# A fused retention and max-out kernel on one core: identity products at the start, decay tables loaded later, and another order of the weight conversion

## Chip, cores, metric

The kernel runs on one core of a Trainium2 chip (trn2). The metric is the device time of one execution in microseconds. Most executions of a kernel agree within 0.3%. The granted clock is the share of TensorE's full clock that the profile or the run's record shows; 1.00 is full. Engines are called TensorE (PE in the profile; PEld are its weight loads), VectorE (DVE), ScalarE (ACT), GpSimd (POOL) and SyncE (SP, which issues most DMAs).

## The reference

```python
# q, k, v: (8, 8, 576, 64) float32
scores = 1 / sqrt(64) * q @ k.transpose(0, 1, 3, 2)
gamma  = 1 - 2.0 ** (-5 - arange(8))                  # one decay per head
ret    = scores * where(i >= j, gamma ** (i - j), 0)  # causal, decaying
x      = (ret @ v).transpose(0, 2, 1, 3).reshape(4608, 512)
h      = maximum(maximum(x @ w1, x @ w2), x @ w3)     # w1..w3: (512, 768)
out    = h @ w_out                                    # w_out: (768, 512)
```

The four weight matrices arrive as float64. The kernel loads their bits as integers and assembles float32 from exponent, mantissa and sign.

## The kernel before

It works through 36 chunks of 128 tokens. Each chunk has three steps: `transposes` (k and q), `scores` (q k^T under a mask, and the running state k^T v), and `values`, which ends in `xT`. The program puts TensorE's results into PSUM tiles, and the copy or product by which another engine takes one out is called its eviction; `st` is that of the masked scores, `xT` that of the output products `o`. Four chunks make one token tile of the max-out layer: 18 "up" products with running maxima, then the "down" products with `w_out`. The first tile runs while the weights are still being converted; `convert(n)` records n steps of a generator, and the order of instructions is manual, so the steps stand on each engine exactly where the program has them.

```python
def conversion(piece):                 # 24 pieces of 128 x 512 weights, four steps each
    expo = wtmp.tile(...); mant = wtmp.tile(...)             # two buffers each
    nc.vector.tensor_scalar(out=expo, in0=high, scalar1=0x7FF00000, op0=bitwise_and)   # mask 1
    nc.scalar.activation(mant, low, Identity, bias=one, scale=2.0 ** -52)
    yield
    nc.scalar.activation(expo, expo, Relu, bias=top, scale=-8.0)
    nc.vector.tensor_scalar(out=frac, in0=high, scalar1=0xFFFFF, op0=bitwise_and)      # mask 2
    yield
    nc.scalar.activation(expo, expo, Relu, bias=inf, scale=-1.0)
    nc.vector.scalar_tensor_tensor(out=mant, in0=frac, scalar=2.0 ** -20, in1=mant, ...)   # mantissa
    yield
    nc.vector.scalar_tensor_tensor(out=expo, in0=high, scalar=-2 ** 31, in1=expo, ...)     # sign
    nc.gpsimd.tensor_tensor(w, mant, expo, op=mult)                                        # product
    load_weights(1)
    yield
# ...
def transposes(g):                     # for the first eight chunks
    # ... TensorE transposes k and q into PSUM, then
            if n == "k" and g < CPT:
                nc.vector.tensor_copy(t[:], pt[:])
            else:
                nc.scalar.copy(t[:], pt[:])
# ... order of the program at the start (the decay tables gk, gq, gs were issued first, on ACT):
load(0); load(1); load(2); load_weights(1); load(3); load_weights(2)
decay_values(0); decay_values(1); transposes(0); transposes(1)
decay_values(2); scores(0); transposes(2); values(0)
decay_values(3); scores(1); convert(4); transposes(3); values(1); scores(2)
load(4); values(2); convert(2); scores(3); decay_values(4); convert(2); values(3); convert(4)
# ... then in the first tile, after each of the 18 up products: convert(5 if n < 4 else 4)
```

## Time and profile before

| | before |
|---|---|
| time at first | 861.55 us median of 3 (860.62 to 861.91) |
| span of the profiled run, TensorE busy | 857.7 us, 844.4 us |
| first up product starts | 31.52 us |
| first down product to the second token block's | 108.94 to 121.36 us |

TensorE is full but for two places, the start and the first down products; the prediction shows the views for that. A line of a timeline gives start and length in us, engine, line of the program (line numbers differ between kernels), operation, tiles, shapes and number of instructions, and in brackets the idle time before it and what ended it. A line of waits gives the total in us, the number and the longest. The end of the start in this profile:

```profile
27.51 1.63 PE L208 MATMUL o<-st,vd 128*64 128x128 f32 x16
...
31.52 7.13 PE L370 MATMUL up<-xT,w 128*128 128x512 f32 x16 [0.42 <-DVE xT L215]
```

Also needed are the groups of instructions on VectorE while the first tile is computed (31 to 116 us). Their columns are line, engine, operation, tiles, shapes and count, then busy time and the mean duration in ns, then the idle time before the group and what ended it.

```profile
L269 DVE TENSOR_SCALAR frac<-bits 128x512 int32<-128x512 int32 x22 | 24.8, 1127 | 0.0
L272 DVE SCALAR_TENSOR_TENSOR mant<-frac,mant 128x512 f32<-128x512 int32 x22 | 15.2, 692 | 2.2
L275 DVE SCALAR_TENSOR_TENSOR expo<-bits,expo 128x512 int32<-128x512 int32 x22 | 15.1, 688 | 4.2 <-ACT expo L271 4.2
L264 DVE TENSOR_SCALAR expo<-bits 128x512 int32<-128x512 int32 x22 | 12.5, 567 | 0.0
```

The two mask groups do the same amount of work and should take the same time. The second takes 1127 ns in the mean instead of some 420: most of that is time in which it is started and cannot run.

### The profile page before, as it was taken

What the parts mean: (1) busy time and instruction counts of PE and PEld (TensorE: products, weight loads), DVE (VectorE), ACT (ScalarE), POOL (GpSimd) and SP (SyncE); (2) the same over time, 40 slices, a digit from 0 to 9 for tenths busy, and PEclk for the clock granted to TensorE, in tenths of its full rate; (3) what the DMA queues carried; (4) which work ended last, traced back from release to release, by engine and by line L of the source; (5) the groups of instructions that cost most, each with busy time, mean ns of one, the idle gap of its engine ahead of it and who ended that gap; (6) DMA issues with size and microseconds to landing.
All of it is one profiled execution on the core that took longest, in us unless ns stands there. A gap on an engine that the chain in (4) does not pass through costs nothing.

```text
span 857.7 us, 11778 instructions
## 1 busy us (share of the span) xinstructions
PE 844.4 (98%) x4320; PEld 614.0 (72%) x4320; DVE 393.6 (46%) x705; ACT 171.4 (20%) x367; POOL 143.3 (17%) x128
## 2 busy tenths in 40 slices
PE   7999989999999999999999999999999999999998
PEld 5645546887588758885788668875888588857883
DVE  4899945654244523444254335442544235432330
ACT  2565631111111102110111111111111011101211
POOL 3534423221210120102011111101111102100000
PEclk9999999999999999999999999999999999999999
DMA  9655531334133323332233213341333223200001
GB/s 245 173 151 160 181 70 43 55 57 85 43 54 56 55 66 66 54 56 61 47 64 68 57 49 56 55 85 45 56 56 54 66 52 66 44 26 24 1 1 49
DMA packets 228409, 59.01 MB, mean 69 GB/s; under 512 B 213504, under 2 KB 222720, under 8 KB 228352
## 3 DMA queue, kind: packets, MB, share of 16 engines
q1 hardware_dynamic: 227920, 57.74, 29.9%
q8 instruction: 34, 0.56, 0.3%
q10 hardware_dynamic: 432, 0.53, 0.2%
q14 instruction: 23, 0.19, 0.1%
HBM read 48.76 MB, written 9.44 MB: 68 GB/s over the span
## 4 chain that ended last, share of the span: by engine, by line
PE 87%; DVE 6%; ACT 4%; issue 1%; DMA 1%; SPq 1%; POOL 0%; DVEq 0%; ACTq 0%
PE x L315 29%; PE down L361 21%; PE z L315 14%; PE y L315 7%; PE s L178 4%; PE o L208 4%; PE o L213 3%; PE kv L189 3%; ACT expo L267 2%; ACT expo L271 1%; DVE expo L275 1%; DVE expo L264 1%; DVE h L375 1%; DVE st L181 1%; DMA kraw<-in_k_dram 1%
## 5 line engine op out<-in xcount | busy, mean ns | idle before, releaser
L361 PE MATMUL down<-wout,h 128*128 128x512 f32 x432 | 190.7, 594 | 3.0 <-POOL wout L278 3.0
L361 PEld LDWEIGHTS down<-wout,h 128*128 128x128 f32 x432 | 80.6, 190 | 95.9 <-issue 90.6
L315 PE MATMUL x<-S,T 128*128 128x256 f32 x576 | 147.9, 379 | 0.0
L148 POOL TENSOR_TENSOR vd<-vraw,gk 128x512 f32<-128x512 f32 x36 | 38.7, 1076 | 499.5 <-DMA vraw<-in_v_dram 483.6
L315 PEld LDWEIGHTS x<-S,T 128*128 128x128 f32 x576 | 109.1, 190 | 15.4 <-ACT u L320 0.3
L181 DVE TENSOR_TENSOR st<-s,causal 128x512 f32<-128x512 f32 x72 | 46.3, 685 | 65.6 <-PE s L178 65.6
L315 PE MATMUL x<-xT,w 128*128 128x256 f32 x288 | 74.8, 382 | 0.0
L315 PE MATMUL x<-S,w 128*128 128x256 f32 x288 | 74.4, 381 | 0.1
L315 PE MATMUL z<-xT,T 128*128 128x256 f32 x288 | 74.0, 379 | 0.0
L315 PE MATMUL z<-S,w 128*128 128x256 f32 x288 | 73.9, 379 | 0.0
L315 PE MATMUL y<-xT,w 128*128 128x256 f32 x288 | 73.9, 379 | 0.0
L320 ACT COPY p<-x 128x256 f32<-128x256 f32 x72 | 26.8, 373 | 220.8 <-PE x L315 217.8
L343 DVE TENSOR_TENSOR tmp<-x,p 128x256 f32<-128x256 f32 x48 | 20.4, 425 | 104.4 <-PE x L315 104.4
L364 ACT COPY osb<-down 128x512 f32<-128x512 f32 x36 | 21.1, 586 | 219.7 <-PE down L361 212.4
L370 PE MATMUL up<-xT,w 128*128 128x512 f32 x144 | 63.5, 594 | 0.4 <-DVE xT L215 0.4
L315 PEld LDWEIGHTS z<-S,w 128*128 128x128 f32 x288 | 54.7, 190 | 7.4
L315 PEld LDWEIGHTS y<-xT,w 128*128 128x128 f32 x288 | 54.7, 190 | 7.4
L315 PEld LDWEIGHTS z<-xT,T 128*128 128x128 f32 x288 | 54.0, 189 | 8.4 <-ACT p L320 0.3
L315 PEld LDWEIGHTS x<-S,w 128*128 128x128 f32 x288 | 49.4, 189 | 13.4 <-issue 1.3
L315 PEld LDWEIGHTS x<-xT,w 128*128 128x128 f32 x288 | 51.5, 190 | 9.6 <-issue 4.2
L215 DVE TENSOR_TENSOR xT<-o,gq 128x512 f32<-128x512 f32 x36 | 24.8, 690 | 69.7 <-PE o L213 63.8
L370 PEld LDWEIGHTS up<-xT,w 128*128 128x128 f32 x144 | 26.7, 190 | 30.9 <-issue 30.1
(64 smaller groups left out, 867.8 us busy)
## 6 DMA issues: line engine op xcount, KB each, us to landing
bits<-in_moe_w_dram SPq DMA_DIRECT2D x18, 512.0 KB, 3.6
out_dram<-osb SPq DMA_DIRECT2D x36, 256.0 KB, 2.0
kraw<-in_k_dram SPq DMA_DIRECT2D x32, 256.0 KB, 3.0
vraw<-in_v_dram SPq DMA_DIRECT2D x32, 256.0 KB, 3.5
qraw<-in_q_dram SPq DMA_DIRECT2D x448, 16.0 KB, 1.9
kxraw<-in_k_dram SPq DMA_DIRECT2D x448, 16.0 KB, 1.8
bits<-in_moe_w_out_dram SPq DMA_DIRECT2D x6, 512.0 KB, 3.5
qraw<-in_q_dram SPq DMA_DIRECT2D x7, 256.0 KB, 4.6
```

Source lines behind the costliest of these rows:

```text
L148: nc.gpsimd.tensor_tensor(t[:], raws.pop(("v", g))[:], gk[:].unsqueeze(2).to_broadcast([C, H, D]), op=ALU.mult)
L178: nc.tensor.matmul(s[j][:, p, :], lhsT=kT[r, p, :], rhs=qT[r, p, :], start=True, stop=True)
L181: nc.vector.tensor_tensor(st[:, j], s[j][:], masks[start_of(g)][:].unsqueeze(1).to_broadcast([C, NP, C]), op=ALU.mult)
L189: nc.tensor.matmul(kv[:, p, :], lhsT=pair(kr, p)[r:], rhs=pair(vds[g], p)[r:], start=True, stop=True)
L208: nc.tensor.matmul(o[D * j:D * (j + 1), p, :], lhsT=vr[:, 2 * p + j, :], rhs=st[:, j, p, :], start=(p == 0), stop=(old == 0 and p == NP - ...
L213: nc.tensor.matmul(o[:, p, :old], lhsT=sd[:, p, :], rhs=qT[:, p, :old], start=False, stop=(p == NP - 1), skip_group_check=True)
L215: nc.vector.tensor_tensor(xT[t][:, :, i * C:(i + 1) * C], o[:], gq[:], op=ALU.mult)
L315: nc.tensor.matmul(out[:], lhsT=w[:, d * P:(d + 1) * P], rhs=xS[t][n][:, d, :], start=first and d == 0, stop=d == 1, skip_group_check=True)
L320: nc.scalar.copy(c[:], src[:])
L361: nc.tensor.matmul(ps[:], lhsT=h[:, fb, m * P:(m + 1) * P], rhs=w_sb["out", fb][:], start=(fb == 0), stop=(fb == NF - 1))
L364: nc.scalar.copy(osb[:], ps[:])
L370: nc.tensor.matmul(ps[:], lhsT=w_sb[i, fb][:, dc * P:(dc + 1) * P], rhs=xT[t][:, dc, :], start=(dc == 0), stop=(dc == NDC - 1))
```

## The change

Its intent is threefold. Identity products keep TensorE busy while the first chunks load, so that its clock is up when they arrive. Two of the three decay tables, which are needed late, no longer stand in front of the first chunks. And the conversion steps are interleaved, with one piece's sign step and product behind the next piece's masks, so that masks do not meet GpSimd's product. Along with that, the copies of the first transposed k go to ScalarE, one more weight buffer is paid for by one raw q buffer, and the `convert` calls are counted anew.

```diff
+    def warm(n):
+        ps = ps_y.tile([P, P], FP32, tag="y", name="warm")
+        for _ in range(n):
+            nc.tensor.matmul(ps[:], lhsT=ident[:], rhs=ident[:], start=True, stop=True)
 # ... in transposes
-            if n == "k" and g < CPT:
-                nc.vector.tensor_copy(t[:], pt[:])
-            else:
-                nc.scalar.copy(t[:], pt[:])
+            nc.scalar.copy(t[:], pt[:])
 # ... the conversion (bodies of the steps as before; "last" is the piece before)
+    def convert_all():
+        last = None
+        for piece in pieces + [None]:
+            # if piece: mask 1 (VectorE); mant (ScalarE)
+            yield
+            # if piece: first Relu (ScalarE); mask 2 (VectorE)
+            yield
+            # if last: sign (VectorE) and product (GpSimd) of the piece before; load_weights(1)
+            # if piece: second Relu (ScalarE)
+            yield
+            # if piece: mantissa (VectorE)
+            yield
 # ... in the first tile, after each up product
-                    convert(5 if n < 4 else 4)
+                    convert(6 if i == 0 else 4)
 # ... the start
-    nc.scalar.dma_start(gq[:], out_decay)          # both were at the very top
-    nc.scalar.dma_start(gs[:], state_decay)
+    warm(9)
     load(0); load(1)
+    nc.sync.dma_start(gs[:], state_decay)
+    nc.sync.dma_start(gq[:], out_decay)
     load(2); load_weights(1); load(3)
-    load_weights(2)
+    load_weights(3); load(4)
     decay_values(0); decay_values(1); transposes(0)
+    warm(5)
     transposes(1)
     # ...
     scores(1)
-    convert(4)
+    convert(2)
     transposes(3); values(1)
+    convert(2)
     scores(2)
-    load(4)
+    convert(3)
     values(2)
-    convert(2)
+    convert(4)
     scores(3)
     decay_values(4)
-    convert(2)
     values(3)
     convert(4)
```

More of the change, by code (lines that the diff above doesn't have):

```diff
@@ L44 @@
 AHEAD = 3
-WAHEAD = 3
+WAHEAD = 4
 @with_exitstack
@@ L132, in load @@
         for n, src in () if g < BY_PE else (("q", q), ("kx", k)):
-            t = raws[n, g] = raw.tile([P, NP, C // 32, 32], FP32, tag=n, name=n + "raw", bufs=4 if n == "q" else 2)
+            t = raws[n, g] = raw.tile([P, NP, C // 32, 32], FP32, tag=n, name=n + "raw", bufs=3 if n == "q" else 2)
             for blk in range(C // 32):
@@ L141, in load @@
         for n, src in rows:
-            t = raws[n, g] = raw.tile([C, H, D], FP32, tag=n, name=n + "raw", bufs=3 if n == "v" else 4)
+            t = raws[n, g] = raw.tile([C, H, D], FP32, tag=n, name=n + "raw", bufs=4 if n == "k" else 3)
             for row, b, pos, m in spans(g):
@@ L241 @@
     pieces = [(i, 2 * fp + e) for fp, i in units for e in range(2)] + [("out", fb) for fb in range(NF)]
-    w_sb, wT, bits = {}, {}, {}
+    w_sb, wT, bits, to_load = {}, {}, {}, deque(pieces)
     def load_weights(n):
         for _ in range(n):
-            if len(bits) == len(pieces):
+            if not to_load:
                 return
-            i, fb = piece = pieces[len(bits)]
+            i, fb = piece = to_load.popleft()
             t = bits[piece] = wraw.tile([P, DM], I64, tag="bits", name="bits")
@@ L254, in load_weights @@
                                   WS[i][:, fb * P:(fb + 1) * P].rearrange("(dc p) f -> p dc f", p=P))
-    def conversion(piece):
-        i, fb = piece
-        words = bits[piece][:].bitcast(I32).rearrange("p (f two) -> p f two", two=2)
-        high = words[:, :, 1]
-        low = bits[piece][:].bitcast(U32).rearrange("p (f two) -> p f two", two=2)[:, :, 0]
-        expo = wtmp.tile([P, DM], I32, tag="expo", name="expo")
-        mant = wtmp.tile([P, DM], FP32, tag="mant", name="mant")
-        nc.vector.tensor_scalar(out=expo[:], in0=high, scalar1=0x7FF00000, scalar2=None, op0=ALU.bitwise_and)
-        nc.scalar.activation(mant[:], low, AF.Identity, bias=one[:], scale=2.0 ** -52)
-        yield
-        nc.scalar.activation(expo[:].bitcast(FP32), expo[:], AF.Relu, bias=top[:], scale=-8.0)
-        frac = wtmp.tile([P, DM], I32, tag="frac", name="frac", bufs=1)
-        nc.vector.tensor_scalar(out=frac[:], in0=high, scalar1=0xFFFFF, scalar2=None, op0=ALU.bitwise_and)
-        yield
-        nc.scalar.activation(expo[:], expo[:].bitcast(FP32), AF.Relu, bias=inf[:], scale=-1.0)
-        nc.vector.scalar_tensor_tensor(out=mant[:], in0=frac[:], scalar=2.0 ** -20, in1=mant[:],
-                                       op0=ALU.mult, op1=ALU.add)
-        yield
-        nc.vector.scalar_tensor_tensor(out=expo[:], in0=high, scalar=-2 ** 31, in1=expo[:],
-                                       op0=ALU.bitwise_and, op1=ALU.bitwise_or)
-        w = w_sb[piece] = const.tile([P, DM], FP32, name=f"w{i}_{fb}")
-        nc.gpsimd.tensor_tensor(w[:], mant[:], expo[:].bitcast(FP32), op=ALU.mult)
-        load_weights(1)
-        yield
@@ new lines, in convert_all @@
+    def convert_all():
+        last = None
+        for piece in pieces + [None]:
+            if piece:
+                raw_bits = bits.pop(piece)
+                words = raw_bits[:].bitcast(I32).rearrange("p (f two) -> p f two", two=2)
+                high = words[:, :, 1]
+                low = raw_bits[:].bitcast(U32).rearrange("p (f two) -> p f two", two=2)[:, :, 0]
+                expo = wtmp.tile([P, DM], I32, tag="expo", name="expo")
+                mant = wtmp.tile([P, DM], FP32, tag="mant", name="mant")
+                nc.vector.tensor_scalar(out=expo[:], in0=high, scalar1=0x7FF00000, scalar2=None, op0=ALU.bitwise_and)
+                nc.scalar.activation(mant[:], low, AF.Identity, bias=one[:], scale=2.0 ** -52)
+            yield
+            if piece:
+                nc.scalar.activation(expo[:].bitcast(FP32), expo[:], AF.Relu, bias=top[:], scale=-8.0)
+                frac = wtmp.tile([P, DM], I32, tag="frac", name="frac", bufs=1)
+                nc.vector.tensor_scalar(out=frac[:], in0=high, scalar1=0xFFFFF, scalar2=None, op0=ALU.bitwise_and)
+            yield
+            if last:
+                (i, fb), h, e, m = last
+                nc.vector.scalar_tensor_tensor(out=e[:], in0=h, scalar=-2 ** 31, in1=e[:],
+                                               op0=ALU.bitwise_and, op1=ALU.bitwise_or)
+                w = w_sb[i, fb] = const.tile([P, DM], FP32, name=f"w{i}_{fb}")
+                nc.gpsimd.tensor_tensor(w[:], m[:], e[:].bitcast(FP32), op=ALU.mult)
+                load_weights(1)
+            if piece:
+                nc.scalar.activation(expo[:], expo[:].bitcast(FP32), AF.Relu, bias=inf[:], scale=-1.0)
+            yield
+            if piece:
+                nc.vector.scalar_tensor_tensor(out=mant[:], in0=frac[:], scalar=2.0 ** -20, in1=mant[:],
+                                               op0=ALU.mult, op1=ALU.add)
+            yield
+            last = piece and (piece, high, expo, mant)
@@ L294, in weight_sums @@
         wT[fp, i] = {1: b11, 2: b21, 3: b22, 4: t4, 5: t1, 6: t2, 7: b12}
-    def convert_all():
-        for piece in pieces:
-            yield from conversion(piece)
     converting = convert_all()
@@ L390, in ffn @@
             yield
-        convert(4 * len(pieces))
+        convert(4 * len(pieces) + 4)
         for m in range(NT // P):
@@ L405 @@
     load(3)
-    load_weights(2)
+    load_weights(3)
+    load(4)
     decay_values(0)
```

## The prediction

> **What bounds the kernel now.** I read the page's busy table first, then the waits of TensorE, then the windows by stage, then the timelines of the two stages where TensorE is not full.
>
> ```profile
> PE 844.4 (98%) x4320; PEld 614.0 (72%) x4320; DVE 393.6 (46%) x705; ACT 171.4 (20%) x367; POOL 143.3 (17%) x128
> ```
>
> TensorE is the bound: it is busy 844.4 us of a span of 857.7. Everything this change can win is inside the other 13.3 us, plus what slow-clocked matmuls hide inside the busy time. The last 3.4 us of the 13.3 (the matmuls end at about 854.2) are the final eviction and store, which the change does not touch. The waits of TensorE, longest first, say where the rest lies:
>
> ```profile
> PE kt L165 <- DMA kraw<-in_k_dram: 4.6, 2, 4.1
> PE down L361 <- POOL wout L278: 3.0, 2, 1.9
> PE qt L165 <- DMA qraw<-in_q_dram: 1.4, 2, 1.2
> PE up L370 <- DVE xT L215: 0.4, 1, 0.4
> PE o L208 <- DVE st L181: 0.2, 1, 0.2
> ```
>
> From 125 us to the end the same view lists no wait of TensorE at all. So only two stages matter: the start (0 to 31.5 us), and the first down products near 110 us. The windows view confirms it (columns: stretch, its length, busy time of PE, PEld, DVE, ACT, POOL, then granted clock, DMA share, GB/s):
>
> ```profile
> 0.00:17.70 17.70, 11.66 (x93) 9.59 (x93) 6.41 (x13) 3.82 (x5) 4.71 (x13) 1.00 0.96 236
> 17.70:31.50 13.80, 13.11 (x132) 10.90 (x132) 11.61 (x20) 4.80 (x7) 8.41 (x6) 1.00 0.62 176
> 31.50:108.90 77.40, 77.38 (x312) 40.24 (x313) 71.60 (x105) 47.91 (x72) 33.91 (x27) 1.00 0.58 168
> 108.90:121.40 12.50, 9.50 (x39) 5.11 (x38) 7.00 (x11) 4.98 (x8) 3.36 (x3) 0.86 0.22 33
> ```
>
> The reader should see three things. Up to 17.7 us the DMA is the full engine (0.96), not TensorE. From 31.5 to 108.9 TensorE is full while VectorE, which converts the weights, is at 71.6 of 77.4 us and falls behind. At 108.9 the bill comes: 3.0 us of waiting for the last two converted weights, and a clock of 0.86. The timeline of TensorE there:
>
> ```profile
> 113.64 1.12 PE L361 MATMUL down<-wout,h 128*128 128x512 f32 x2 [1.10 <-POOL wout L278]
> 116.67 1.45 PE L361 MATMUL down<-wout,h 128*128 128x512 f32 x2 [1.90 <-POOL wout L278]
> 118.04 2.08 PE L178 MATMUL s<-qT,kT 64*128 64x128 f32 x16
> 120.05 1.48 PE L189 MATMUL kv<-vd,kraw 128*128 128x128 f32 x8
> ```
>
> The sixteen score matmuls take 2.08 us here against 1.16 us in the same view at 64.36, when TensorE had been full.
>
> **What the Trainium skill says.** (1) "TensorE: Matmul & The Clock Gate", Part 1: TensorE runs at half rate until it has been busy through a window of about 3.4 us, and falls back after an idle one. The trace agrees in durations: four transposes are paced 0.90 us at 9.14 and 0.44 us at 12.95 in the chain, and the scores double after the waits near 115. It also shows that the granted clock printed for 0 to 17.7 us (1.00) does not reveal the slow start. (2) "SBUF — State Buffer", section "SBUF: two separate sides": VectorE and GpSimd share a port pair as an exclusive lock; VectorE in a two-port mode, or with two SBUF inputs, fully blocks against GpSimd. The trace agrees, with the price beside it, first VectorE's timeline:
>
> ```profile
> 29.11 1.76 DVE L275 SCALAR_TENSOR_TENSOR expo<-bits,expo 128x512 int32<-128x512 int32 x1
> ...
> 41.66 0.42 DVE L264 TENSOR_SCALAR expo<-bits 128x512 int32<-128x512 int32 x1
> 42.00 1.50 DVE L269 TENSOR_SCALAR frac<-bits 128x512 int32<-128x512 int32 x1
> ```
>
> and from GpSimd's timeline of the same stretch:
>
> ```profile
> 41.83 1.39 POOL L278 TENSOR_TENSOR w<-mant,expo 128x512 f32<-128x512 f32 x1 [1.76 <-DVE expo L275]
> ```
>
> The same mask costs 0.42 us free and 1.50 us across a GpSimd product. The sign step (two SBUF inputs) takes 0.68 us normally and 1.76 across GpSimd's state product. Steps that read PSUM (scores, maxima) keep 0.68 us beside GpSimd. (3) "Trainium Kernel Development and Optimization", Key Constraints: DMAs of all queues run on the same 16 engines, so another queue adds no bandwidth. The 0.96 share fits.
>
> **The change part by part.**
>
> Decay factors later. Two 256 KB loads leave the front and stand behind v of chunk 1. Before, chunk 0's q reached TensorE at 6.37 us and chunk 1's k at 8.03 us. From v1 at 10.5 us back to v0 at 7.16 us I read 1.1 us for 256 KB, so both come about 2 us earlier. But chunk 3's q is still behind the same fifteen 256 KB units (k, q, v of chunks 0 to 2, two decay tables, one 512 KB weight piece, k3, q3), and the DMA is full. It stays at about 17.6 us, where TensorE already waited for it (0.21 us). So the gain is hidden again before 18 us: worth 0.
>
> Identity products. Nine before the first transposes, each two records, at about 0.23 us when slow (0.90/4): some 4 us, from 1.5 to 5.5 or 6 us. That covers the 4.1 us wait and delays chunk 0's transposes by up to 2 us, which the earlier data and faster clock repay: I put the first kv product's end at about 12.3 us instead of 12.95. Five more cost 1.4 to 2.3 us where TensorE would wait anyhow. All of it ends at the same q3 wait: worth 0 at 18 us. The kT copies (four at 0.68 us) leave VectorE for ScalarE, which has room.
>
> Conversion order, long stage. A piece needs two masks (0.42 each), two SBUF steps (0.68 each), some 2.0 us paced, and a 1.27 us product on GpSimd. Before, a piece with its maximum cost 3.87 us (from 76.67 to 80.54, with only 0.6 of it the maximum), as VectorE also waits for ScalarE's two steps and one mask meets the product. In the new order the sign step and product of one piece follow the next piece's masks, so ScalarE is never waited for. With a maximum behind the product, half of the product runs beside a PSUM step: maximum 0.6, mantissa until about 1.9 (product end 1.35, plus 0.55 as after 30.32), masks 0.7, sign 0.6, about 3.2 us. Where three pieces follow each other it stays near 3.3 us, because the mantissa step also has two SBUF inputs. Per three units of ups: 6 x 3.2 plus 1.9 + 0.6 attention in the two i>0 units is less than TensorE's time, and only the i=0 unit (9.9 us against 7.0 + attention) lags and recovers. So VectorE keeps pace: the last sign step falls 1 to 2.5 us after the downs start, the last weight is ready by 3 to 3.8 us, and it is needed 5 x 0.86 = 4.3 us after. The waits vanish. From down start to the second down the trace has 121.36 - 108.94 = 12.42 us; without wait at full clock six downs (5.15), scores (1.09) and kv (1.09) take 7.33. **Gain 5.1 us** if nothing is left of the wait.
>
> Conversion order, start. Fifteen conversion steps instead of twelve stand before the first up product, and more of them in front of the third chunk's mask (the order of instructions on VectorE shows sign, xT, mantissa, two masks, sign between state 2 and scores 3). From 23.6 us, paced: mask 0.35, mask blocked by GpSimd's state product to 25.5, sign 26.1, xT 26.7, mantissa blocked by the first weight product to 28.05, masks 28.7, sign 29.3, then the scores' evictions to 30.5. Before they ended at 28.0. TensorE's last output product then starts near 30.5 instead of 27.5 to 28, its first up product at about 33.5 instead of 31.52. **Loss about 2 us**, and perhaps 0.5 more if the 3 us gap lets the clock fall (the gaps of 1.1 and 1.9 us near 113 did).
>
> Sum: 861.55 - 5.1 + 2.0 + 0.5 = 858.95. Since my schedule of the start is hand-made and leans to the pessimistic side, I shade it to **858.5 us** (ratio 0.9965).
>
> **Rivals.** (a) The start gains instead: TensorE's pure work from q3 to the first up product is about 11.7 us, so without VectorE in its way ups could start at 29.9, 1.6 us earlier: 855. Against it: the blocked steps counted above. (b) VectorE still finishes late, because lock and mantissa step only swap victims: part of the 3.0 us wait and of the slow clock stay, 860 to 862. For it: 3.3 us for pieces in a row is no better than the 3.14 us now (38.52 to 41.66). (c) Nine slow identity products delay chunk 0 beyond what the DMA hides: at most 1 us more. (d) The larger weight ring and smaller q ring change transfers: the DMA share is 0.58 in that stage, so I give this nothing.
>
> **Range and chances.** Down stage -5.1 in most outcomes, -2 at worst; start between -1.6 and +3.5: 80% of that lies in 855.0 to 862.0. A 2% gain needs 844 us, the busy time of TensorE itself; a 2% loss needs 17 us of new waits. Both are nearly excluded.
>
> **What would show it.** Right: no wait of down for wout; scores after the first downs at 1.16 us and clock 1.00 there; still a q3 wait near 17.6 with a first transpose after 5 us; the wait of o for st of 2 to 3 us near 28 to 30; the first up at 33 to 34; the first-mask rows back to 0.42 us and the mantissa step lengthened to 1.2 or more. Wrong: q3 landing well before 17 us, the first up before 31 us, or a wout wait that survives.

## The result

The changed kernel took 858.79 us (median of 4 runs, 858.12 to 859.14); the kernel before took 861.73 us beside it (4 runs, 860.62 to 862.91). Ratios are the mean time of one kernel's runs over that of the other's of the same rounds, so not quite the ratio of the medians quoted. Here the ratio is 0.9965, with a 95% interval of 0.9947 to 0.9982: a small gain.

TensorE's waits in the changed kernel, over the whole span:

```profile
PE o L209 <- DVE st L182: 2.5, 2, 2.4
PE warm L109 <- POOL ident masks.py:199: 1.4, 1, 1.4
PE qt L169 <- DMA qraw<-in_q_dram: 1.0, 2, 0.8
PE kt L169 <- DMA kraw<-in_k_dram: 0.8, 2, 0.5
```

The 3.0 us of down products waiting for converted weights are gone. In their place stands a wait that was 0.2 us before: output products wait 2.5 us for masked scores. The timeline of TensorE shows both places:

```profile
30.64 0.43 PE L209 MATMUL o<-st,vd 128*64 128x128 f32 x2 [2.37 <-DVE st L182]
31.23 1.80 PE L209 MATMUL o<-st,vd 128*64 128x128 f32 x14 [0.17 <-DVE st L182]
32.97 2.05 PE L214 MATMUL o<-qT,state 128*128 128x128 f32 x8
...
35.89 4.53 PE L377 MATMUL up<-xT,w 128*128 128x512 f32 x10
...
113.28 5.32 PE L368 MATMUL down<-wout,h 128*128 128x512 f32 x12
118.53 1.16 PE L179 MATMUL s<-qT,kT 64*128 64x128 f32 x16
```

The twelve down records now run without a break, and the scores behind them take 1.16 us instead of 2.08. But after the 2.37 us gap near 28 to 30 us the clock is down: the state products take 2.05 us instead of 1.16, and the window from 31.20 to 34.85 us has a granted clock of 0.53. The first up product starts at 35.89 us, 4.4 us later than in the first profile of before.

Why the masked scores come late, on VectorE's timeline:

```profile
24.70 1.50 DVE L275 TENSOR_SCALAR frac<-bits 128x512 int32<-128x512 int32 x1
26.13 0.68 DVE L279 SCALAR_TENSOR_TENSOR expo<-bits,expo 128x512 int32<-128x512 int32 x1
26.73 0.68 DVE L216 TENSOR_TENSOR xT<-o,gq 128x512 f32<-128x512 f32 x1
27.33 1.38 DVE L288 SCALAR_TENSOR_TENSOR mant<-frac,mant 128x512 f32<-128x512 int32 x1
...
29.90 1.28 DVE L182 TENSOR_TENSOR st<-s,causal 128x512 f32<-128x512 f32 x2
```

Conversion steps stand in front of the eviction `st`, two of them (1.50 and 1.38 us) lengthened by GpSimd's products. And the groups of VectorE during the first tile (31 to 118 us):

```profile
L288 DVE SCALAR_TENSOR_TENSOR mant<-frac,mant 128x512 f32<-128x512 int32 x22 | 17.9, 814 | 0.2 <-ACT mant L270 0.2
L279 DVE SCALAR_TENSOR_TENSOR expo<-bits,expo 128x512 int32<-128x512 int32 x22 | 15.1, 687 | 0.0
L269 DVE TENSOR_SCALAR expo<-bits 128x512 int32<-128x512 int32 x21 | 10.0, 475 | 9.3 <-POOL w L282 8.2 <-POOL wout L282 1.2
L275 DVE TENSOR_SCALAR frac<-bits 128x512 int32<-128x512 int32 x21 | 8.8, 421 | 0.0
```

The second mask is back at 421 ns. The first mask takes 475 ns, but 9.3 us of idle time have appeared in front of it, ended by GpSimd. Idle time included, the two masks of a piece cost 1.34 us in the mean instead of 1.70, and the idle time before the mantissa and sign steps fell from 6.4 us to 0.2, while the mantissa step grew from 692 to 814 ns.

### The profile page after: what moved, and what is told of

The parts are those of the page before. It is cut to its first block, busy times and chain, and to the rows that moved or that the text cites. A ratio compares the mean times of both kernels' runs of the same rounds, so it can differ in the third digit from the quotient of the medians.

```text
span 857.1 us, 11859 instructions
## 1 busy us (share of the span) xinstructions
PE 847.5 (99%) x4348; PEld 618.8 (72%) x4348; DVE 376.5 (44%) x701; ACT 175.3 (20%) x371; POOL 145.6 (17%) x128
## 4 chain that ended last, share of the span: by engine, by line
PE 95%; DMA 1%; DVE 1%; SPq 1%; issue 0%; ACT 0%; DVEq 0%; ACTq 0%
PE x L322 29%; PE down L368 22%; PE z L322 14%; PE up L377 7%; PE y L322 7%; PE o L209 4%; PE s L179 4%; PE o L214 4%; PE kv L190 3%; DMA qraw<-in_q_dram 1%; SPq L148 1%; DMA kraw<-in_k_dram 0%; SPq L142 0%; PE qt L169 0%; PE kt L169 0%
## 5 line engine op out<-in xcount | busy, mean ns | idle before, releaser
L377 PEld LDWEIGHTS up<-xT,w 128*128 128x128 f32 x144 | 26.7, 190 | 30.5 <-issue 30.3
```

The source lines that it names most:

```text
L377: nc.tensor.matmul(ps[:], lhsT=w_sb[i, fb][:, dc * P:(dc + 1) * P], rhs=xT[t][:, dc, :], start=(dc == 0), stop=(dc == NDC - 1))
```

## The experiments

All eleven kernels gave correct results. Times are medians; "before" beside them was 861.1 to 861.8 us.

### 1. Four conversion steps moved from in front of chunk 3's masked scores

```diff
     values(2)
-    convert(4)
     scores(3)
     decay_values(4)
     values(3)
-    convert(4)
+    convert(8)
```

> The changed kernel with one move: the four conversion steps that stand on VectorE in front of chunk 3's masked scores go behind chunk 3's values. Theory (the start of the changed kernel lost 4.4 us, of which 2.4 us are the wait of the output products for those masked scores, and some 1.7 us the slow clock that this gap brings): the wait falls under 0.5 us, the eight state products after it are back from 2.05 to 1.16 us, the first up product starts at 32 to 32.5 us instead of 35.9, and the time falls by 3 to 4 us to about 855. Rival (the start lost its time to the identity products and the later q of chunk 3): the first up product stays at 35 us or later and the time within 1 us of 858.8.

Measured: 853.96 us (4 runs), ratio 0.9913 (0.9900 to 0.9927). TensorE's timeline in this run:

```profile
28.19 1.54 PE L209 MATMUL o<-st,vd 128*64 128x128 f32 x16
29.66 1.16 PE L214 MATMUL o<-qT,state 128*128 128x128 f32 x8
...
31.70 7.20 PE L377 MATMUL up<-xT,w 128*128 128x512 f32 x16
```

The wait is gone, the state products take 1.16 us, and the first up product starts 4.2 us earlier than in the changed kernel. The time fell by 4.8 us by the medians of two sessions, and by 4.4 when each kernel is taken against the kernel before beside it: somewhat more than the 3 to 4 expected. The rival fails: identity products and the later q are still in this kernel, so they did not cost the 4 us. The place of the four steps in VectorE's order cost them.

### 2. The conversion order alone

The kernel before with the new conversion, its buffer sizes and counts; the first-tile steps are aligned by `convert(7)` instead of `convert(4)` after `values(3)`.

> The kernel before with the new conversion order and its four raw buffers alone; decay factors first, no identity products, transposed k copied as before, and the steps at the start kept off the masked scores as before. Theory: the waits of the first down products for the last converted weights (3.0 us) and the slow clock after them vanish, from down start to the second down 7.3 us instead of 12.4, so about 856.5 (5 us below before). Rival (the gain comes from the start, by identity products and earlier first chunks): 860 or more, with waits for converted weights left.

Measured: 856.97 us (5 runs), ratio 0.9947 (0.9935 to 0.9960). The stage from down start to the second token block takes 7.34 us (111.24 to 118.58), as the theory has it. The order was not tested apart from the fourth weight buffer; but in the kernel before, between 31 and 109 us, VectorE waited for no weight piece and ScalarE 0.2 us for one, so a buffer alone had little to win. One new wait appears, in TensorE's waits:

```profile
PE up L376 <- POOL w L281: 1.9, 1, 1.9
```

The first up product's weight was late: its sign step sat behind chunk 3's state, and on GpSimd its product queued behind a state product and a value product. So this part is worth 5.1 us at the downs of these profiles, and 4.4 us by the medians. The first up product starts at 33.82 us, level with the 33.76 of experiment 4's profile; without the 1.9 us wait it would start earlier.

### 3. The start's parts alone

Identity products, late tables, and k's copies on ScalarE, with the old conversion.

> The kernel before with the start's parts alone: identity products, two decay tables behind chunk 1, k's transposed copy on ScalarE; the old conversion order. Theory: TensorE still meets q of chunk 3 at 17.6 to 18.6 us, so the first up product is at 31 to 32.5 us and the time 861 to 862.5, no gain over before. Rival (warming and earlier data are worth their 2 to 3 us): 859 or less, first up product before 30 us.

Measured: 859.95 us (5 runs, 858.82 to 861.03), ratio 0.9983 (0.9970 to 0.9995): a gain of about 1.4 us, between theory (none) and rival (2 to 3); the first up product starts at 32.59 us. The theory of "worth nothing" is therefore not quite right; experiments 5 to 8 look for the source.

This run's profile also shows the down stage with both waits (1.14 and 1.89 us), and yet:

```profile
118.83 1.16 PE L180 MATMUL s<-qT,kT 64*128 64x128 f32 x16
```

Nearly the same gaps as in before, but no slow clock after them. That the cost varies from run to run also fits the record: two of this kernel's five runs have a mean granted clock of 1.000 (858.82, the profiled one, and 859.34 us), one has 0.998 (859.95) and two have 0.996 (860.87 and 861.03), while the nine of before beside it have 0.998 or 0.996. So part of the 1.4 us may be luck with the clock.

### 4. The kernel before again

> The kernel before itself, unchanged, as a null run and for a second profile of it. Its profiled run was 859.4 us while its timed runs were 860.6 to 862.9. Theory (the length of the slow clock after a wait varies from run to run): ratio 1.000 within 0.002, and a profile in which the stage from down start to the second down, or the start, differs by 1 us or more from the first profile. Rival (both stages repeat to 0.3 us): then the 2 us lie outside of what the profile shows.

Measured: 861.54 us (5 runs), ratio 1.000 (0.9986 to 1.0013). Its profile, of a run of 861.54 us, differs from the first in the start. TensorE's waits from 15 to 35 us:

```profile
PE kv L189 <- DVE kT L168: 1.0, 1, 1.0
...
```

and the first up product on TensorE's timeline:

```profile
33.76 6.70 PE L370 MATMUL up<-xT,w 128*128 128x512 f32 x15 [0.42 <-DVE xT L215]
```

Here q of chunk 0 came at 6.94 us instead of 6.37, TensorE was slow until 13 us, and VectorE's copy of chunk 3's k stood behind conversion steps that were blocked (a mantissa step of 1.57 us), so by the profile the kv product waited 1.0 us for it. The first up product started at 33.76 us instead of 31.52. The down stage repeated: 12.48 us (111.18 to 123.66) against 12.42. So the first profile (a run of 859.42 us) caught a start that was about 2 us better than most: the timed runs beside it took 860.62 us or more. A comparison with the changed kernel is fairer with this second profile.

### 5 to 7. The kernel of experiment 1 without identity products, with the tables first, with both undone

```diff
-    warm(9)                                  # runs 5 and 7
-    warm(5)                                  # runs 5 and 7
+    nc.scalar.dma_start(gq[:], out_decay)    # runs 6 and 7, at the top again
+    nc.scalar.dma_start(gs[:], state_decay)
-    nc.sync.dma_start(gs[:], state_decay)    # runs 6 and 7
-    nc.sync.dma_start(gq[:], out_decay)
```

> The kernel of the first experiment without the identity products. Theory (what they win before 18 us is lost at the wait for q of chunk 3): 854.0 within 0.7, that wait shorter than 0.7 us, the first up product at 31.7 within 0.7. Rival (they are worth the slow clock's cost of some 2.5 us on the first transposes and scores): 855.5 or more.

> The kernel of the first experiment with the two decay tables first on ScalarE's queue again. Theory (the fifteen 256 KB units ahead of chunk 3's q are the same in either order): 854.0 within 0.7. Rival (the two tables ahead delay chunks 0 and 1 by about 2 us that are not made up): 855.5 or more.

> The kernel of the first experiment with neither identity products nor late decay tables; of the start's parts only k's transposed copies on ScalarE stay. Theory (with both gone TensorE reaches chunk 3 about when its q lands, so little is left; the 1.4 us that the start's parts won in their own run come mostly from VectorE being rid of k's copies, one of which held the kv product for 1.0 us in the second profile of before): 854 to 855. Rival (the two parts only help together): 855.5 or more, with TensorE reaching chunk 3's transposes after its q has landed.

| kernel | us (median) | ratio to before | first up product |
|---|---|---|---|
| experiment 1 | 853.96 | 0.9913 (0.9900 to 0.9927) | 31.70 us |
| no identity products | 854.08 | 0.9922 (0.9909 to 0.9936) | 32.02 us |
| tables first | 854.53 | 0.9933 (0.9920 to 0.9947) | 31.58 us |
| both undone | 853.71 | 0.9922 (0.9909 to 0.9936) | 31.05 us |

The intervals overlap (experiment 1 ran in other rounds, so compare ratios), the three rivals of 855.5 us or more failed, and the kernel with both undone is as fast as any, 0.3 us below its theory's 854 to 855. Its TensorE is later at chunk 0 and slow until about 13 us (chunk 0's scores take 2.08 us from 10.10 us), and yet it comes to chunk 3's q at 17.97 us, without a wait for it:

```profile
17.97 0.60 PE L171 MATMUL qt<-ident,qraw 128*128 128x128 f32 x4
```

Experiment 1 reaches q of chunk 3 earlier, waits 0.73 us, and starts those transposes at 18.59 us. Whatever the identity products and the table order win in the first 13 us is lost at that wait. An effect of a few tenths of a microsecond cannot be seen in these runs.

### 8. k's copies on ScalarE alone

The kernel before with nothing but the changed copy in `transposes`.

> The kernel before with one change, the copies of the first four chunks' transposed k on ScalarE instead of VectorE. Theory (the start's parts won 1.4 us in their own run, and identity products and late tables win nothing in the runs without them, so it is this): 859.7 to 860.5, no wait of the kv product for a copy of k. Rival (the two other parts win it when VectorE's conversion order is the old one): 861 or more.

Measured: 860.52 us (5 runs), ratio 0.9985 (0.9972 to 0.9998), practically that of all the start's parts together (0.9983); the kv product's wait for k's copy is absent from its waits (0.6 us of waits of `o` for `st` stand in its place). Here the clock does not explain the gain: four of the five runs have the mean granted clock of 0.998 that all nine of before beside them have, and their median is 860.6 against 861.8 us. So the 1.3 us of the start's parts are most likely this one line, though the interval ends only just below 1 and the start's parts without it were not run. It is not the part that the change is named after. What it is worth with the new conversion order was not tested; experiment 2, with k's copies on VectorE, shows no wait for them.

### 9 and 10. Chunk 3's loads ahead of the first weight piece

```diff
     load(2)
-    load_weights(1)
     load(3)
-    load_weights(3)
+    load_weights(4)
```

Run 9 does this to experiment 1. Run 10 does it to the kernel with both undone, and spreads the first conversion steps: four behind `scores(2)`, three behind `scores(3)`.

> The kernel of the first experiment (four conversion steps behind chunk 3's values) with chunk 3's loads ahead of the first 512 KB weight piece. Theory (q of chunk 3 sets the pace of the start once nothing of VectorE is in the way): q of chunk 3 reaches TensorE at about 16.7 us instead of 18.6, the first up product starts near 30 us instead of 31.7, and the time is 1 to 2 us below 853.96, about 852.5. Rival (VectorE, whose first mask then waits for the later weight piece, or the weights of the first up products, become the wait): the first up product does not move or waits for a converted weight, time 853.5 to 855.

> The kernel with the moved steps and the old front (853.71), with chunk 3's loads ahead of the first weight piece and the first conversion steps spread so that none stands in front of an eviction before its weight piece has landed: four behind chunk 2's scores, three behind chunk 3's. Theory (in the run with chunk 3's loads first, VectorE's first mask waited for the later weight piece and held TensorE for 1.2 us; without that the earlier q is worth 0.5 to 1 us): 852.7 to 853.3, no wait of scores for an eviction. Rival (the first weights then come too late for the first up product, behind the state and value products on GpSimd): first up product waits for a converted weight by 1 us or more, 854 or more.

Both rivals held. Run 9: 854.85 us, ratio 0.9932 (0.9920 to 0.9944). Chunk 3's transposes ran at 16.77 us (k) and 17.21 us (q), but the first mask then waited for the weight piece, on VectorE's timeline:

```profile
19.23 1.29 DVE L269 TENSOR_SCALAR expo<-bits 128x512 int32<-128x512 int32 x1 [1.46 <-DMA bits<-in_moe_w_dram]
```

`xT` of chunk 1 stood behind it, TensorE's scores waited 1.16 us, by the profile for that eviction, and the first up product started at 31.79 us, no earlier. Run 10: 856.42 us, ratio 0.9941 (0.9927 to 0.9954); its up products waited 1.9 us in two waits for converted weights. In run 9 the mask that waited for a late DMA held up `xT`, which stood behind it on VectorE, until 20.77 us. So loads and the order of their first uses must be moved together.

### 11. A third exponent buffer

```diff
-                expo = wtmp.tile([P, DM], I32, tag="expo", name="expo")
+                expo = wtmp.tile([P, DM], I32, tag="expo", name="expo", bufs=3)
 # paid for by two buffers instead of three for raw q
```

> The changed kernel with three buffers instead of two for the exponent tile (paid for by two buffers instead of three for raw q). In the changed kernel, where three pieces follow each other, the next piece's first mask stands idle for 1.17 us until GpSimd's product is done, because it writes the buffer which that product reads. Theory (the port pair is taken as a whole for one instruction, so the buffer only decides where the time is booked): the idle time before the first mask (9.3 us in all between 31 and 118 us) falls under 2 us, its mean duration rises from 475 to 800 ns or more, the mask rows there grow to about 1.5 us, a piece still takes 3.1 us, and the time stays at 858.8 within 1. Rival (the dependence on the buffer is what costs, masks run beside the product): masks stay at 0.42 us, the idle time goes, and a piece shrinks to 2.2 us or less; the time may still not move, as VectorE is not the bound there.

Measured: 858.86 us (4 runs), ratio 0.9966 (0.9950 to 0.9983), as the changed kernel. First masks on VectorE where pieces follow each other, and the group of the first mask:

```profile
65.48 1.50 DVE L269 TENSOR_SCALAR expo<-bits 128x512 int32<-128x512 int32 x1
...
68.60 1.50 DVE L269 TENSOR_SCALAR expo<-bits 128x512 int32<-128x512 int32 x1
```

```profile
L269 DVE TENSOR_SCALAR expo<-bits 128x512 int32<-128x512 int32 x21 | 16.3, 777 | 0.0
```

The idle time before the mask went from 9.3 us to none, its mean duration from 475 to 777 ns (a little under the 800 expected), and from mask to mask it is still 3.12 us (65.48 to 68.60) and 2.96 us for the next. So in the changed kernel it is the shared buffer, not the order alone, that keeps the first mask off the product, and that is bookkeeping: the mask pays about the same time as a wait or as a blocked instruction. In the terms of the Trainium skill ("SBUF — State Buffer", "SBUF: two separate sides"), the port pair that VectorE and GpSimd share is an exclusive lock; this run agrees, with 1.50 us against 0.42.

## Why the prediction was right, point by point

The predicted 858.5 us was measured as 858.79. Most of the mechanism held. One term of the sum was mis-sized, and the baseline hid that.

- **Downs, -5.1 us.** Right. From down start to the second token block it is 7.34 us (113.28 to 120.62) against 12.42 and 12.48 in the two profiles of before, and experiment 2 shows it without the other parts. The last sign step ended at 114.5 us, 1.2 us after the downs started, within the 1 to 2.5 predicted. About 1.5 us of the 5.1 are the slow clock, which not every run pays: in experiment 3's profile, with the same waits, the stage took 10.90 us (110.01 to 120.91).
- **Conversion pace.** Right in size: where three pieces follow each other a piece takes 3.13 us (65.40 to 68.53), predicted 3.3 and no faster than the 3.14 of before, as rival (b) had it. The gain lies where the masks no longer meet the product and in the idle time before the mantissa and sign steps (above). Partly wrong in detail. I expected the mantissa step to grow to 1.2 us or more; it grew only to 814 ns in the mean. Where pieces follow each other it starts first (63.55 us), so GpSimd's product (from 63.71 us) is the one that is held (1.66 us instead of 1.27), and the next first mask waits 1.17 us for that product.
- **Identity products and late tables, 0.** Right: experiments 5 to 7. I had taken q of chunk 3 at 17.6 us from one profile; with the tables late TensorE got it at 18.6 to 19.1 us. (Of the prediction's fifteen units the last is q itself; fourteen stand in front of it.) I had given k's copies no value; experiment 8 finds about 1.3 us, by taking VectorE's blocked steps out of k's way.
- **Start, +2.0 and +0.5 us.** Right in place and cause: the wait of output products for masked scores was predicted as 2 to 3 us and is 2.5. **Mis-sized as a sum.** The first up product was predicted at 33 to 34 us and came at 35.89. The failing term is the stretch from the last output product, predicted near 30.5 us and measured at 30.64, to the first up product: I gave it 3.0 us, and 0.5 for the clock. It takes 3.51 us at full clock (experiment 1, 28.19 to 31.70) and took 5.25 us here. Against the profile that I used, the first up product came 4.4 us later (35.89 against 31.52), not 2.5. It was 0.9 us for the later q of chunk 3 (18.59 against 17.67, put at 0) and 3.45 us from there on (17.30 against 13.85): 2.37 us of wait, about 1.6 us of slow clock (1.80 and 2.05 us against 1.09 and 1.16; I had put 0.5), less the 0.42 us wait for `xT` that went away.
- **The baseline.** That error did not show because I subtracted from the timed median of 861.55 us, while working from a profile of a run of 859.42 us, whose start was some 2.2 us faster than in the second profile. Against the second profile, whose run is as long as the timed ones and where q of chunk 3 starts at 18.66 us, the start loses 2.1 us (35.89 against 33.76) and the downs win 5.1: -3.0 us, and the medians differ by 2.94. The close hit owes part of itself to two errors of about 2 us that cancel: that part was luck.

The rivals: (a), the start gains instead, became true only with experiment 1, where the first up product came 2.1 us before that of before's second profile (and 0.2 us after that of the first). (b), VectorE still late at the downs, did not happen, although lock and mantissa step did swap victims. (c) was nothing: chunk 0's transposes started at 5.44 us, and chunk 3 still waited. (d) was nothing too: the DMA share while the first tile's up products run is 0.57 (35.9 to 113.3 us), before 0.58.

The best kernels are experiment 1 and the one with both parts undone, about 7.4 us (0.8 to 0.9%) faster than before: the new conversion order, k's copies on ScalarE, and no conversion step between chunk 2's values and chunk 3's masked scores. Further from the bound there is little: TensorE is busy 845.4 of 852.4 us in experiment 1.

## What to carry to other kernels

When background work shares an in-order engine with evictions that TensorE waits for, place each of its steps by asking which eviction stands behind it. Here the same four steps cost 4 us in front of one eviction, and nothing that can be seen behind the values that follow it. Take two profiles of the baseline before sizing effects of 2 us, since one run can be lucky in its start, and look at each run's granted clock. And check each named part alone: here two of the three contributed nothing measurable, and an unadvertised copy gave most likely more than both.

## What the Trainium skill lacked or had wrong

- "TensorE: Matmul & The Clock Gate", Part 1 and the table under "Why this matters for your kernels", speak of idle gaps over some 3 us. Here shorter ones sufficed: after a gap of 2.37 us the granted clock was 0.53 for 3.65 us (experiment 11 repeats it: 2.36 us, then state products of 2.08 us), and after gaps of 1.10 and 1.90 us with 1.12 us of matmuls between them the scores took 2.08 us. It is not certain either: with 1.14 and 1.89 us (experiment 3) they took 1.16. So where the prediction says that the trace agrees with Part 1, it agrees on the halved rate, not on the length of the idle time.
- The same page, Part 4, says of transposes that the full clock does not engage for them. Here four transposes took 0.60 us behind busy stretches and 1.09 us at the start, so they do run faster when the clock is up. Whether transposes alone bring the clock up, no run here shows.
- "TensorE: Matmul & The Clock Gate", Part 1, warns that recorded clock events can be unreliable. Neither it nor another page that I read says that the granted clock of a window can read 1.00 while TensorE is slow at the beginning of a program: 0 to 17.7 us in before, with transposes at 1.09 us against 0.60.
